# Moving the second chunk's transposes from TensorE to DMA in a fused FFT-mixing and gated-MLP kernel, with two alternating token buffers

## The chip, the cores and the metric

One core of a Trainium2 chip. The metric is the device time of one execution in microseconds (us). An execution that is over 1.5% longer than the fastest of the same kernel in its round is called slow, the others fast: of 15 executions of the kernel before, 12 took 181.61 to 183.95 us and three 184.34 to 186.31 us. Where a profiled execution was itself a slow one, the text says so, and only its local order of events is read from it.

## The reference, cut to what matters

```python
def reference(A_x, A_w_r, A_w_i, B_x, B_w_gate, B_w_up, B_w_down):
    x = A_x                                    # 1 x 2048 x 512, bf16
    xn = _layernorm(x, axis=-1)
    # A: irfft2(rfft2(xn) * (w_r + 1j * w_i));  weights 2048 x 257
    # B: (gelu(xn @ w_gate) * (xn @ w_up)) @ w_down;  512 x 1792 and 1792 x 512
    return x + _A_ref(xn, A_w_r, A_w_i) + _B_ref(xn, B_w_gate, B_w_up, B_w_down)
```

The kernel writes both Fourier transforms as matrix products in stages: a 512-point stage along the features, then 64-point and 32-point stages along the tokens, a product with the filter, and the same backwards. Gate, up and down products of the MLP fill TensorE between these stages.

## The kernel before: the parts that the change and the argument touch

The 2048 tokens are worked on as four chunks of 512. Each chunk is normalised (VectorE, with a power on GpSimd), transposed into `xnT`, combined by four additions and subtractions ("butterflies", VectorE) and multiplied by the 512-point table (`unit_D`, TensorE). The gate and up products need the same `xnT`. Between the 64-point and the 32-point stage each chunk is written to a scratch in DRAM and loaded back (`scr`, `tv`), both by SP's queue.

```python
def trans(m, dcs, jjs, eng="dve"):        # on TensorE: 8 transposes into a PSUM bank, then a copy
    bk = take(1, 0.45, 1.2)
    ...
def trans_dma(m):                         # one DMA transpose of 128 x 2048 fp16 (0.5 MB), SP's queue
    op("sp", lambda e: e.dma_start_transpose(xnT[...], xn...),
       r=[("xn", i) for i in range(4)], w=[("xnT", m, dc, jj) ...], dma=True)
```

Side work hangs on numbered hooks between the gate and up units; a hook is passed after each group of four 128x512 matmuls (0.86 us) and after each product. Loads of constants and weights hang there too, by default on GpSimd's queue:

```python
def load_late(dst, src, keys, also=(), eng="pool"):
    op(eng, lambda e: e.dma_start(dst, src), ..., dma=True, after=[("pe", pr.cnt["pe"])])
...
for i in range(4):                                    # down weights, 1.8 MB
    at(10 + 2 * i, (load_late, wd_sb[...], wdv[...], ...))
at(18, (load_late, be[:], c_be.ap(), ["be"]))         # two small tables
at(19, (load_late, mm[:], c_mm.ap(), ["mm"]))
for s, h0 in enumerate((24, 31, 38, 53, 61, 66, 70, 75)):   # eight sets of filter rows,
    for i, t in enumerate(load_W(s)): at(h0 + i // 2, t)    # half by GpSimd's queue, half by SP's
    at(89 + s // 2 if s > 3 else (47, 48, 51, 58)[s], (keep_256, s))
```

PSUM banks are chosen while the program is built, from an estimate of when each comes free; the choice is fixed in the built kernel:

```python
def take(n, dur, hold=None, ops=1):       # n neighbouring banks
    i = min(range(9 - n), key=lambda i: max(free[i:i + n]))
    ...
```

In the second half, eight groups of 32-point work alternate a unit `unit_B` and `unit_C`.

## Time and profile before

| before | value |
|---|---|
| time, median of 3 | 183.42 us (182.3 to 186.33) |
| span of the profiled execution, granted clock | 181.5 us, full speed in every slice |
| second chunk: transposes | 16 on TensorE, two blocks of 0.46 us, near 25 and 26 us |
| third and fourth chunk: DMA transposes, issue to landing | 7.7 us (issued at 34.74), 6.3 us (46.42) |
| first matmul of the third and fourth chunk's 512-point stage | 44.51 and 54.79 us, late by 1.45 and 0.96 us |
| first 32-point unit; first unit after the eight groups | 74.20; 122.22 us |

How to read it: TensorE sets the end; it is busy for 173.2 of the 181.5 us. A wait of it in the first 55 us is taken to move the end by its own length (my estimate: its row has no gap worth naming behind that), and so the two late stages, with the transposes on TensorE, are what the change goes for.

### The profile page before, as it was taken

The page shows a single profiled execution, that of the slowest core. Times are in us where ns is not written, and L with a number is a line of the kernel's source. Part 1 is how long each engine was busy: PE and PEld are TensorE (multiplying, and loading weights), DVE is VectorE, ACT ScalarE, POOL GpSimd, SP SyncE. Part 2 cuts the span into 40 slices and gives each one's busy share as a digit, 9 for nine tenths or more (in the row PEclk, how much of TensorE's full clock was granted, in tenths as well). Part 3 has the DMA queues.
Part 4 walks back from the last instruction along what each step waited for, and adds up shares of the span by engine and source line. Part 5 has one row for each costly group of instructions (what it writes and reads, how often), then busy time and mean ns, then how long its engine had stood idle before and what let it go on. Part 6 is the DMA issues. An engine that isn't in the chain of part 4 may idle for free.

```text
span 181.5 us, 3815 instructions
## 1 busy us (share of the span) xinstructions
PE 173.2 (95%) x1406; PEld 107.9 (59%) x1406; DVE 132.4 (73%) x331; ACT 93.9 (52%) x158; POOL 54.9 (30%) x107
## 2 busy tenths in 40 slices
PE   7889999997989999999999999999999999999992
PEld 2478654553536556556655656556676767666882
DVE  3496989966649695786876649797877777897552
ACT  3334547763666631475655755336858677632110
POOL 2210171462222426186570000001354625640000
PEclk9999999999999999999999999999999999999999
DMA  3999998698999566469973121394155755552104
GB/s 86 320 270 304 342 280 297 169 234 148 242 167 207 132 158 164 115 166 205 216 188 92 58 61 58 106 249 170 19 99 105 130 115 101 92 86 44 29 5 116
DMA packets 31059, 27.89 MB, mean 154 GB/s; under 512 B 7120, under 2 KB 27984, under 8 KB 30912
## 3 DMA queue, kind: packets, MB, share of 16 engines
q1 hardware_dynamic: 26016, 19.88, 44.6%
q0 software_dynamic: 4272, 7.24, 18.2%
q10 hardware_dynamic: 752, 0.52, 1.1%
q8 instruction: 11, 0.18, 0.4%
q14 instruction: 8, 0.07, 0.1%
HBM read 18.19 MB, written 6.29 MB: 135 GB/s over the span
## 4 chain that ended last, share of the span: by engine, by line
PE 70%; DVE 12%; DMA 11%; SPq 2%; issue 2%; POOL 1%; ACT 0%; DVEq 0%
PE ps L778 23%; PE ps L889 19%; PE ps L874 18%; DMA xnT<-cmx 8%; DMA wu<-in_B_w_up_dram 4%; DVE st L384 3%; SPq L337 2%; PE ps L604 2%; PE ps L632 2%; PE ps L832 2%; DVE hT L895 2%; PE ps L579 2%; DVE cmx L430 1%; DVE arena L740 1%; DVE arena L434 1%
## 5 line engine op out<-in xcount | busy, mean ns | idle before, releaser
L889 PE MATMUL ps<-xnT,wu 128*128 128x512 f16 (+1 forms) x248 | 58.4, 359 | 0.7 <-DMA wu<-in_B_w_up_dram 0.7
L874 PE MATMUL ps<-xnT,wg 128*128 128x512 f16 (+1 forms) x248 | 58.4, 359 | 0.5 <-ACT xnT L1023 0.5
L877 ACT ACTIVATE gl<-ps 128x512 bf16<-128x512 f32 (+1 forms) x62 | 34.4, 556 | 37.5 <-PE ps L874 36.7
L895 DVE TENSOR_TENSOR hT<-ps,gl 128x512 bf16<-128x512 f32 (+1 forms) x62 | 39.2, 635 | 19.9 <-PE ps L889 13.9
L889 PEld LDWEIGHTS ps<-xnT,wu 128*128 128x128 bf16 x248 | 23.1, 98 | 20.4 <-issue 1.2
L874 PEld LDWEIGHTS ps<-xnT,wg 128*128 128x128 bf16 x248 | 23.2, 98 | 15.8 <-issue 1.4
L340 POOL DMA_DIRECT2D wring<-in_A_w_r_dram x32 | 18.4, 609 | 18.1 <-PE ps L874 7.7
L641 POOL COPY tv<-tv 1x128 bf16<-1x128 bf16 x16 | 5.4, 338 | 41.9 <-ACT tv L639 41.8
L778 PE MATMUL ps<-wd,hT 128*128 128x256 bf16 x112 | 14.4, 273 | 0.0
L858 POOL DMA_DIRECT2D x_sb<-tv x16 | 13.2, 865 | 3.4 <-DVE tv L851 2.4
L384 DVE BATCH_NORM_STATS2 st<-x_sb 128x6 f32<-128x512 bf16 x16 | 10.5, 680 | 3.9 <-DMA x_sb<-in_A_x_dram 3.9
L455 ACT ACTIVATE early<-ps 128x512 f16<-128x512 f32 x16 | 9.5, 595 | 7.2 <-PE ps L451 7.2
L590 DVE TENSOR_TENSOR early<-early,wring 128x1024 bf16<-128x1024 f16 x16 | 10.3, 686 | 3.8 <-ACT early L585 3.8
L797 ACT ACTIVATE ps<-ps 128x256 f32<-128x256 f32 x16 | 5.9, 369 | 13.2 <-PE ps L778 13.1
L778 PEld LDWEIGHTS ps<-wd,hT 128*128 128x128 bf16 x112 | 10.7, 98 | 2.5
L392 POOL TENSOR_TENSOR rstd<-vpe,mhalf 128x4 f32<-128x4 f32 (+2 forms) x6 | 5.0, 837 | 21.2 <-DVE vpe L391 21.2
L778 PE MATMUL ps<-arena,xnT 128*128 128x256 f16 x91 | 11.4, 273 | 0.0
L838 ACT ACTIVATE tv<-ps 128x512 bf16<-128x512 f32 x16 | 9.5, 595 | 3.6 <-PE ps L832 3.6
L639 ACT ACTIVATE tv<-ps 128x512 bf16<-128x512 f32 x16 | 9.5, 595 | 3.2 <-PE ps L632 3.2
L585 ACT ACTIVATE early<-ps 128x1024 f16<-128x1024 f32 x8 | 8.2, 1023 | 4.8 <-PE ps L579 4.8
L778 PEld LDWEIGHTS ps<-arena,xnT 128*128 128x128 f16 x91 | 8.6, 98 | 2.3 <-DVE tw L801 0.3
L659 DVE TENSOR_TENSOR x_sb<-ps,tw 128x256 bf16<-128x256 f32 x16 | 6.7, 421 | 2.9 <-PE ps L778 2.6
(118 smaller groups left out, 236.9 us busy)
## 6 DMA issues: line engine op xcount, KB each, us to landing
wring<-in_A_w_r_dram POOLq DMA_DIRECT2D x32, 64.2 KB, 4.0
wring<-in_A_w_i_dram SPq DMA_DIRECT2D x32, 64.2 KB, 3.9
tv<-scr SPq DMA_DIRECT2D x8, 256.0 KB, 5.0
scr<-early SPq DMA_DIRECT2D x8, 256.0 KB, 2.2
wring<-scr SPq DMA_DIRECT2D x4, 512.0 KB, 7.1
x_sb<-tv POOLq DMA_DIRECT2D x16, 128.0 KB, 2.8
scr<-early SPq DMA_DIRECT2D x15, 128.0 KB, 3.5
out_dram<-x_sb SPq DMA_DIRECT2D x28, 64.0 KB, 2.0
```

Source lines behind the costliest of these rows:

```text
L340: op(eng, lambda e: e.dma_start(dst, src), w=list(keys) + list(also), dma=True, after=[("pe", pr.cnt["pe"])])
L384: op("dve", lambda e: e.bn_stats(st[:, j, :], x_sb[:, j, :]), r=[("x", j, 0), ("x", j, 1)], w=[("st", j)])
L455: op("act", lambda e: e.activation(x4.rearrange("p (a c r) -> p a c r", a=2, r=4), bank(bk).rearrange("p (a r c) -> p a c r", a=2, r=4), A ...
L590: op("dve", lambda e, k=k: e.tensor_tensor(pp[i][k], xc[i], W[k][g % 4][:, :, :, 0:256], ALU.mult), r=[("xc", i)] + [key for c in range(2) ...
L639: op("act", lambda e: e.activation(z, bank(bk).rearrange("p (a c) -> p a c", a=4), ACT.Copy, scale=SC_E), r=[("ps", bk)], w=[zk] + (TVK if ...
L778: ins = e.matmul(o, st_(f), mv(f), start=(f == 0 and step in (0, 5)), stop=(f == 6), skip_group_check=True)
L838: op("act", lambda e: e.activation(o2, bank(bk), ACT.Copy), r=[("ps", bk)], w=[ok] + (TVK if j < 2 else []))
L858: op("pool", lambda e: e.dma_start(x_sb[:, j, :], ys, accum_op=ALU.add), r=[yk + (0,), yk + (1,), ("x", j, 0), ("x", j, 1)] + acc(j), w=ac ...
L874: ins = e.matmul(bank(bg)[:, 0:n], wg_sb[:, dc, fc * P:(fc + 1) * P], xnT[:, j0:j0 + len(jjs), dc, :], start=(dc == 0), stop=(dc == 3))
L877: op("act", lambda e: e.activation(gl[k % 3][:, 0:n], bank(bg)[:, 0:n], ACT.Gelu_apprx_tanh), r=[("ps", bg)], w=[("gl", k % 3)])
L889: ins = e.matmul(bank(bu)[:, 0:n], wu_sb[:, dc, fc * P:(fc + 1) * P], xnT[:, j0:j0 + len(jjs), dc, :], start=(dc == 0), stop=(dc == 3))
L895: op("dve", lambda e: e.tensor_tensor(hT[b % 2][:, fc, h0:h0 + n], bank(bu)[:, 0:n], gl[k % 3][:, 0:n], ALU.mult), r=[("ps", bu), ("gl", k ...
```

## The change

The second chunk is transposed by DMA as well. Since the transposes are now closer together, the third chunk is normalised into a second buffer (`twh`, space that is free until later), so that its normalisation needn't wait until the second chunk's transpose has read the first buffer. Each chunk's 512-point stage is moved to the hook where its transpose is expected to have landed: the second chunk's from hook 22 to 27, the third's from 31 to 35, the fourth's from 39 to 40. Two small moves come along: the third filter set from hook 38 to 37, and one 32-point unit (`unit_C` of the fourth group) a hook later.

```diff
+        def xnb(m):
+            return twh.rearrange("p (a d) -> p a d", a=4) if m == 2 else xn
...
         def trans_dma(m):
-            op("sp", lambda e: e.dma_start_transpose(xnT[...], xn.rearrange("p a d -> p (a d)")),
+            op("sp", lambda e: e.dma_start_transpose(xnT[...], xnb(m).rearrange("p a d -> p (a d)")),
...
-        for s, h0 in enumerate((24, 31, 38, 53, 61, 66, 70, 75)):
+        for s, h0 in enumerate((24, 31, 37, 53, 61, 66, 70, 75)):
...
         for m in range(1, 4):
-            a = (5, 15, 23)[m - 1]
-            t = (16, 25, 33)[m - 1]
+            a = (5, 15, 22)[m - 1]
+            n = (10, 20, 27)[m - 1]
+            t = (20, 29, 36)[m - 1]
...
-                at(a + 5 + i // 2, (ln_norm, 4 * m + i))
-            if m < 2:
-                at(t, (trans, m, (0, 1), (0, 1, 2, 3)))
-                at(t + 1, (trans, m, (2, 3), (0, 1, 2, 3), "act"))
-            else:
-                at(a + 6, (trans_dma, m))
+                at(n + i // 2, (ln_norm, 4 * m + i))
+            at(n + 1, (trans_dma, m))
...
-            h = (11, 22, 31, 39)[m]
+            h = (11, 27, 35, 40)[m]
...
-                at(h + (g in (1, 5)), (unit_C, g - 1))
+                at(h + (g in (1, 4, 5)), (unit_C, g - 1))
```

More of the change, by code (lines that the diff above doesn't have):

```diff
@@ L304, in bass_parallel_sum__spectral_gfnet__glu_gated_geglu__prompt_kernel @@
         tw = sb("tw", [P, 2, 512], F32)
+        twh = tw[:].rearrange("p a c -> p (a c)").bitcast(F16)
         dumm = sb("dumm", [P, 512], F16)
@@ L393, in ln_aggr, with xnk @@
                w=[("rstd", j) for j in js])
+        def xnb(m):
+            return twh.rearrange("p (a d) -> p a d", a=4) if m == 2 else xn
+        def xnk(m, a):
+            return ("tw", a // 2, a % 2 == 0) if m == 2 else ("xn", a)
         def ln_norm(j):
-            op("dve", lambda e: e.tensor_scalar(xn[:, j % 4, :], x_sb[:, j, :], ag[:, j, 0:1], rstd[:, j:j + 1], ALU.subtract, ALU.mult),
-               r=[("x", j, 0), ("x", j, 1), ("ag", j), ("rstd", j)], w=[("xn", j % 4)])
+            op("dve", lambda e: e.tensor_scalar(xnb(j // 4)[:, j % 4, :], x_sb[:, j, :], ag[:, j, 0:1], rstd[:, j:j + 1], ALU.subtract, ALU.mult),
+               r=[("x", j, 0), ("x", j, 1), ("ag", j), ("rstd", j)], w=[xnk(j // 4, j % 4)])
         def trans(m, dcs, jjs, eng="dve"):
@@ L419, in trans_dma @@
         def trans_dma(m):
-            op("sp", lambda e: e.dma_start_transpose(xnT[:, 4 * m:4 * m + 4].rearrange("p j d c -> p (j d) c"), xn.rearrange("p a d -> p (a d)")),
-               r=[("xn", i) for i in range(4)], w=[("xnT", m, dc, jj) for dc in range(4) for jj in range(4)], dma=True)
+            op("sp", lambda e: e.dma_start_transpose(xnT[:, 4 * m:4 * m + 4].rearrange("p j d c -> p (j d) c"), xnb(m).rearrange("p a d -> p (a d)")),
+               r=[xnk(m, i) for i in range(4)], w=[("xnT", m, dc, jj) for dc in range(4) for jj in range(4)], dma=True)
         def butter(m, part):
@@ L712, in sum_01 @@
                    after=readers(home + (SK(3) if k == 1 else [])))
-        twh = tw[:].rearrange("p a c -> p (a c)").bitcast(F16)
         def s01k(b, p, k):
```

## The prediction

> **What bounds the kernel now.** I read the page first (busy shares, then the 40 slices), then the chain of waits, then TensorE's timeline and, beside it, those of VectorE and of the SP queue from 12 to 66 us, then the transfers by window.
>
> ```profile
> PE 173.2 (95%) x1406; PEld 107.9 (59%) x1406; DVE 132.4 (73%) x331; ACT 93.9 (52%) x158; POOL 54.9 (30%) x107
> ...
> PE   7889999997989999999999999999999999999992
> ...
> DMA  3999998698999566469973121394155755552104
> ```
>
> TensorE is busy nearly everywhere. From slice 13 (about 55 us) on it has no gap worth naming, so a microsecond saved before that moves the end by a microsecond. What can be saved lies in slices 3 to 12. The DMA row is full up to slice 6, about 32 us. That matters below.
>
> ```profile
> 25.16 0.62 PE L406 MATMUL ps<-ident,cmx 128*128 128x128 f16 x8 [0.24 <-DVE cmx L396]
> ...
> 26.48 0.61 PE L406 MATMUL ps<-ident,cmx 128*128 128x128 f16 x8
> ...
> 42.20 1.03 PE L889 MATMUL ps<-xnT,wu 128*128 128x512 f16 x4
> 44.51 0.23 PE L447 MATMUL ps<-fd,arena 128*128 128x128 f16 x1 [1.28 <-DVE arena L434]
> ...
> 54.79 0.23 PE L447 MATMUL ps<-fd,arena 128*128 128x128 f16 x1 [0.79 <-DVE arena L434]
> ```
>
> In TensorE's timeline (start, length, instruction, idle before it) L406 are the 16 transposes of the second chunk of tokens, L447 the first matmul of a chunk's 512-point stage. Both stages whose tokens come by DMA make TensorE wait. The listed idle is short of the wait, because the pipelined ends are modelled. I use the distance between starts: four 128x512 matmuls start their successor 0.86 us later (41.34 to 42.20), so the unit of 42.20 is done at 43.06, and 44.51 is 1.45 us late.
>
> ```profile
> 34.74 3.39 SPq L420 DMA_TRANSPOSE xnT<-cmx  x1
> ...
> 46.42 2.27 SPq L420 DMA_TRANSPOSE xnT<-cmx  x1
> ```
> ```profile
> 42.49 0.69 DVE L430 TENSOR_TENSOR cmx<-xnT 128x1024 f16<-128x1024 f16 x1 [2.85 <-DMA xnT<-cmx]
> ...
> 52.77 0.69 DVE L430 TENSOR_TENSOR cmx<-xnT 128x1024 f16<-128x1024 f16 x1 [2.58 <-DMA xnT<-cmx]
> ```
>
> So the cause is plain: a DMA transpose takes 7.7 and 6.3 us from its issue, VectorE idles for it, then needs 2.0 us for four butterflies (42.49 to 44.51), and TensorE arrives before that is done.
>
> [...]
>
> **The change, part by part.** I number the places where the program hangs its side work ("hooks"), one after each gate or up unit (four matmuls, 0.864 us) and after each product, and put each on TensorE's timeline.
>
> Removed from TensorE: the transposes. Two blocks of 8 cost 0.46 us each (25.16 to 25.62), 0.91 in all; the first also waited for the normalised tokens (unit of 23.89 done at 24.75, transposes at 25.16), 0.41. From VectorE go 0.67 us, from ScalarE 1.02 us, both then off the path.
>
> Removed by moving: the two waits, 1.45 us before 44.51, and 0.96 before 54.79 (the unit of 52.97 is done at 53.83). The second chunk's own stage waited 0.22 (32.66 to 32.88). Sum of all that can go: 0.91 + 0.41 + 1.45 + 0.96 + 0.22 = 3.95 us. A further 0.27 us wait at 66.8, for a difference of weights on VectorE, may go too, as its producers come earlier relative to TensorE; at most 4.2 us. VectorE's and GpSimd's work for normalisation is the same; only its destination changes for the third chunk.
>
> Now each stage against its transpose, on a timeline without waits. After 24.75 TensorE reaches hook 20 at 28.5, hook 27 at 35.65, hook 35 at 45.0 and, behind the third chunk's 64-point stage, hook 40 at 51.7.
>
> Third chunk: VectorE has its tokens at about 32.7; SP is free at about 33.1 (its four scratch writes took 2.82 us and come a little over 1 us earlier). Plus 7.7 us gives 40.8. Butterflies hang at hooks 31 and 32 (40.4 and after), done near 44.2; the matmuls at 45.0 find them ready. The wait of 1.45 goes. Its own buffer frees nothing else early: the fourth chunk's normalisation comes at hook 27 anyway.
>
> Fourth chunk: tokens near 41.1, landing near 48 to 49, butterflies at hook 38 (48.6) and 39, done near 51.4, against 51.7. No wait, or a few tenths.
>
> Second chunk: tokens at 25.02, as before. The transpose is issued at 25.1, into this:
>
> ```profile
> 25.00:26.00 1.00, 0.84 (x10) 0.66 (x11) 1.00 (x3) 0.55 (x1) 1.00 (x2) 1.00 1.02 251
> ...
> 30.00:31.00 1.00, 1.00 (x18) 0.72 (x18) 1.00 (x2) 0.95 (x2) 0.00 (x0) 1.00 0.94 315
> 31.00:32.00 1.00, 1.00 (x5) 0.42 (x6) 0.97 (x7) 1.00 (x2) 0.35 (x1) 1.00 0.32 109
> ```
> ```profile
> x_sb<-in_A_x_dram SPq DMA_DIRECT2D x1, 256.0 KB, 15.0
> ```
>
> The last two columns of the windows are the DMA share and GB/s: full until 31. The second fence is the first of the last two input loads of SP, issued at 13.84, landing at 28.8; the two have a median of 13.2, so the other took 11.4 and lands near 29.8. In front of the new transpose SP's queue is full until then, and GpSimd's 1.8 MB of down weights (issued from 23.1, landing 8 to 9 us later) take their share. In the two old cases the transpose landed 4.3 to 4.9 us after the scratch writes ahead of it (last issues near 34 and 44.3, 3.6 us each). From 29.8 that gives an estimate of 34.1 to 34.7; with the plain 7.7 it would be 32.8. I take 34.0. After it VectorE runs, by program order, two butterflies (1.28), a statistic (0.60), a product for the up unit (0.60) and the last two butterflies (0.75): 3.2 us, so 37.2, against TensorE's arrival at 35.65. **New wait: about 1.5 us**, in a range of 0.3 to 2.2.
>
> The later stages then slide by the same time on both engines, so it is counted once. Sum: 4.1 - 1.5 = 2.6 us, and a few tenths of noise. 183.42 - 2.7 = **180.7 us**, a ratio of 0.985.
>
> **Rivals.** (a) The third transpose is hidden: it lands by 32.5 and VectorE, busy until 32.7, never waits. For it: the author put 17 hooks between normalisation and matmuls here against 13 and 15 elsewhere, as if measured. Against: the full DMA row. It would give 179.3 to 179.5, just beyond 2%. (b) The queue behind the loads is worse, landing at 36 or later: the gate units of the second chunk, which need the same tokens at hook 27, wait as well, and since VectorE is in order, up products pile up behind the butterflies (it lags TensorE by 3 to 4.4 us already between 17 and 26 us), PSUM banks stay taken, and the gain falls to 1 us or less: 182.5 or more. For it: the input loads took 15 us in this queue. Against: most of their bytes are gone by 25. (c) The gain moves to a later wait: the second half needs the scratch reload of the fourth chunk by hook 59. Before, it was issued at 67.5, landed near 71.4, used at 74.2, 2.8 us to spare. After, the stage is one hook later in the program but SP carries fewer loads ahead of it; I estimate 1 to 2 us to spare. If not, 1 us is lost.
>
> **Range and chances.** The ceiling of 4.2 us is 2.3%, so faster by over 2% needs a new wait under 0.5 us: (a), 0.2. Slower by over 2% would need a loss of over 7 us, for which no part is big enough, or a disturbed run: 0.03. The rest is within 2%. The range is 179.2 (all gone, a lucky run) to 182.3 (b, or a and c together with the spread of 182.3 to 186.3 of the kernel before).
>
> **What would show it.** In the changed kernel: no L406 after 14 us; three DMA transposes on SP, the first at 25.1 landing after 8 to 9.5 us, the others after 6 to 8; VectorE idle 1 to 2 us before the second chunk's first butterfly; TensorE's only wait of over 0.5 us between 20 and 60 us before the second chunk's first 512-point matmul, near 36 to 37; the third and fourth stages without one. Wrong if the first landing is at 32.7 or before (then a), if TensorE's units slow down with no tokens awaited (b), or if a wait appears at the 32-point stage near 70 us (c).

## The result, and the profile after

The changed kernel took 191.76 us (median of 4, 190.42 to 196.62) against 183.31 us for the kernel before on the same chip: a ratio of 1.0465 (95% interval 1.0357 to 1.0574). It is slower by over 2%, outside the predicted range. All ratios here are worked out from the fast runs of both kernels in the same rounds, so they are not quite the ratio of the medians quoted.

The first profiled execution was a slow one (span 194.7 us), so the changed kernel was run again unchanged, as the run r1_again below, whose profiled execution was fast (span 187.9 us). Everything said of the kernel after is read from that one. Its page, 40 slices of 4.7 us:

```profile
PE   7799999509999999999999999999999999999991
...
PEclk9999999965999999999999999999999999999998
DMA  4999999995668856739774212186064665651104
```

There is one hole in TensorE's row, at slices 7 and 8 (counted from 0), where there was none before; in its second half and right behind it, in slices 8 and 9, the granted clock is lowered. The trace's record of the clock has half speed from 39.44 to 46.27 us. The end of TensorE's timeline around it (start, length, instruction, idle before it and what ended it; L455 is the first matmul of a chunk's 512-point stage):

```profile
34.60 1.03 PE L895 MATMUL ps<-xnT,wu 128*128 128x512 f16 x4
41.99 0.29 PE L455 MATMUL ps<-fd,arena 128*128 128x128 f16 x1 [6.36 <-DVE arena L442]
...
42.60 1.91 PE L880 MATMUL ps<-xnT,wg 128*128 128x512 f16 x4
44.31 0.31 PE L455 MATMUL ps<-fd,arena 128*128 128x128 f16 x1
...
46.47 0.22 PE L455 MATMUL ps<-fd,arena 128*128 128x128 f16 x1
```

By the prediction's own measure, the unit of 34.60 is done at 35.46, so the second chunk's stage is 6.53 us late. And the four matmuls at 42.60 take 1.71 us until their successor starts, instead of 0.86. From 41.99 to 46.47 there are two pairs of a 512-point unit and a gate or up unit, 1.19 us each at full clock (before: 45.72 to 46.91); 4.48 - 2.38 = 2.10 us are lost to the lowered clock. The table by windows has the clock itself (third column from the end):

```profile
42.00:44.00 2.00, 2.00 (x8) 1.05 (x9) 2.00 (x4) 0.60 (x1) 0.00 (x0) 0.50 0.95 252
```

What TensorE waits for is VectorE's last butterfly (L442), and VectorE waits for the transpose. First VectorE's timeline, then the SP queue's:

```profile
38.77 0.69 DVE L438 TENSOR_TENSOR cmx<-xnT 128x1024 f16<-128x1024 f16 x1 [6.08 <-DMA xnT<-cmx]
...
41.51 0.42 DVE L442 TENSOR_TENSOR arena<-cmx 128x512 f16<-128x512 f16 x1
```
```profile
24.93 6.61 SPq L428 DMA_TRANSPOSE xnT<-cmx  x1
...
35.33 4.95 SPq L428 DMA_TRANSPOSE xnT<-tw  x1
...
47.36 1.62 SPq L428 DMA_TRANSPOSE xnT<-cmx  x1
```

The transpose of 24.93 landed 13.8 us after its issue, the other two after 6.9 and 4.4 us. From its landing on, all runs as predicted: 3.2 us of VectorE, and the stage begins. The third chunk's stage waits for nothing. The fourth's is about 0.3 us late (its first matmul is at 60.40, with 0.23 us of listed idle); in return a wait of 0.27 us that the kernel before had near 66.5 us is gone, and the two cancel in the sum below.

The whole difference, by the times of the same events in both traces:

| from before to after | us |
|---|---|
| transposes off TensorE (0.91) and old waits gone (0.41 + 1.45 + 0.96 + 0.22) | -3.95 |
| first 512-point gate unit begins earlier in this execution (19.78 to 19.57) | -0.21 |
| new wait before the second chunk's stage | +6.53 |
| lowered clock after it | +2.10 |
| sum: first 32-point unit at 74.20 before, 78.67 after | +4.47 |
| eight 32-point groups: 48.02 before (74.20 to 122.22), 49.12 after (78.67 to 127.79) | +1.10 |
| from there to the last product group: 54.44 in both | 0 |
| after VectorE's last instruction (3.1 before, 3.9 after), not followed up | +0.8 |
| sum: span 181.5 to 187.9 | +6.4 |

The gain came as computed, but for the 0.3 us at the fourth stage. Three things ate it: a landing 4.8 us later than the 34.0 predicted, the clock, and 1.1 us in a place that the change seemed hardly to touch.

### The profile page after: what moved, and what is told of

Read it like the earlier page. It is cut to its first block, busy times and chain, and to the rows that moved or that the text cites. A ratio compares the mean times of both kernels' runs of the same rounds, so it can differ in the third digit from the quotient of the medians.

```text
span 194.7 us, 3785 instructions
## 1 busy us (share of the span) xinstructions
PE 175.4 (90%) x1390; PEld 108.3 (56%) x1390; DVE 132.3 (68%) x330; ACT 93.1 (48%) x157; POOL 53.8 (28%) x107
## 4 chain that ended last, share of the span: by engine, by line
PE 75%; DMA 14%; DVE 4%; SPq 2%; issue 2%; ACT 2%; DVEq 0%
PE ps L784 22%; PE ps L895 21%; PE ps L880 21%; DMA xnT<-cmx 9%; DMA wu<-in_B_w_up_dram 5%; SPq L338 2%; PE ps L612 2%; PE ps L640 2%; PE ps L838 2%; PE ps L587 1%; ACT early L593 1%; DVE hT L901 1%; PE ps L458 1%; PE ps L459 1%; PE ps L455 1%
## 5 line engine op out<-in xcount | busy, mean ns | idle before, releaser
L895 PE MATMUL ps<-xnT,wu 128*128 128x512 f16 (+1 forms) x248 | 59.3, 363 | 1.8 <-DMA wu<-in_B_w_up_dram 1.8
L880 PE MATMUL ps<-xnT,wg 128*128 128x512 f16 (+1 forms) x248 | 59.4, 363 | 1.3 <-DMA wg<-in_B_w_gate_dram 0.7
L784 PE MATMUL ps<-wd,hT 128*128 128x256 bf16 x112 | 14.4, 273 | 0.0
L455 PE MATMUL ps<-fd,arena 128*128 128x128 f16 x16 | 3.8, 236 | 10.1 <-DVE arena L442 10.1
L593 ACT ACTIVATE early<-ps 128x1024 f16<-128x1024 f32 x8 | 8.2, 1022 | 4.8 <-PE ps L587 4.8
```

Source lines behind the costliest of these rows:

```text
L593: op("act", lambda e: e.activation(xc[i].rearrange("p r hh c -> p (r hh c)"), pair(bk), ACT.Copy, scale=SC_B), r=[("ps", bk), ("ps", bk + ...
L784: ins = e.matmul(o, st_(f), mv(f), start=(f == 0 and step in (0, 5)), stop=(f == 6), skip_group_check=True)
L880: ins = e.matmul(bank(bg)[:, 0:n], wg_sb[:, dc, fc * P:(fc + 1) * P], xnT[:, j0:j0 + len(jjs), dc, :], start=(dc == 0), stop=(dc == 3))
L895: ins = e.matmul(bank(bu)[:, 0:n], wu_sb[:, dc, fc * P:(fc + 1) * P], xnT[:, j0:j0 + len(jjs), dc, :], start=(dc == 0), stop=(dc == 3))
```

## The experiments

The question for the first five runs: why did a transpose that takes 4 to 8 us elsewhere take 13.8 us here? The main theory: while a transpose's packets and those of another queue's loads are in flight together, the transpose hardly moves; here GpSimd's down weights (issued from 22.86 on) and the loads behind them are the others. The rivals: the transpose only waits its turn behind SP's own input loads, or one particular load does it, or the moved stages themselves are badly placed.

**r1_again: the change unchanged**, for a fast profile and as the base of the others.

> The change once more, unaltered, for a second trace beside the runs that follow. If its slowness is steady: 190 to 192 us, the first DMA transpose landing 13 us or more after its issue while GpSimd's queue carries the down weights and small loads, TensorE waiting 6 us or more and its granted clock then at 0.5 for some microseconds. If the first trace was an odd one: a landing within 9 us in this trace.

Measured: 190.81 us, ratio 1.0349 (1.0272 to 1.0426); two of the four runs were fast. Its profile is the one above. (r2 to r5 were run before it; their expectations quote the slow first execution, in which TensorE waited 9.9 us.) The record of DMA transfers by window gives the first piece of evidence. From 27 to 29 us (queue, kind: packets, MB, share of the 16 engines' time; then the transpose with its time to landing):

```profile
q0 software_dynamic: 178, 0.66, 98.6%
q1 hardware_dynamic: 7, 0.02, 4.0%
...
xnT<-cmx SPq DMA_TRANSPOSE x1, 13.8
```

q0 is GpSimd's queue, q1 SP's. For two microseconds, 2 us after the transpose was issued, GpSimd's queue has the engines nearly for itself. The seven packets of q1 are not yet the transpose's: five have 4096 bytes and two have 4, the rest of SP's input loads, which landed at 28.34 and 29.31 us. The transpose's own packets, 2048 of 256 bytes, start between 29.65 and 35.81 us (in r11, below, between 27.09 and 30.09). From 29.6 to 32 us, beside the down weights, three packets in five are the transpose's, but they are so small that they carry 0.08 of 0.75 MB:

```profile
q0 software_dynamic: 202, 0.67, 92.7%
q1 hardware_dynamic: 314, 0.08, 18.9%
```

From 33.0 to 34.2 us hardly anything moves in either queue (161 packets of q1, 12 of q0), and why is open. From 34.2 to 35.2 us the transpose has the engines to itself, and half of it passes in this one microsecond:

```profile
q1 hardware_dynamic: 1035, 0.26, 125.4%
```

**r2_second_on_pe: the second chunk back on TensorE**, all the rest of the change kept.

```diff
-            t = (20, 29, 36)[m - 1]
+            t = (16, 29, 36)[m - 1]
-            at(n + 1, (trans_dma, m))
+            if m < 2: (the two blocks of transposes of the kernel before)
+            else:     at(n + 1, (trans_dma, m))
-            h = (11, 27, 35, 40)[m]
+            h = (11, 22, 35, 40)[m]
```

> The second chunk goes back to TensorE transposes at its old places; the third and fourth keep the change's buffer and later stages. If the whole loss comes from the second chunk's DMA transpose, the old waits of 1.45 and 0.96 us before the third and fourth chunk's stages are gone and no new one appears: 181.0 us (ratio 0.987). If moving the stages or the second buffer costs something by itself: 184 or more.

Measured: 185.2 us, ratio 1.0039 (0.9987 to 1.0092). So the loss belongs to the second chunk's transpose by DMA, not to the moved stages. But these alone gain nothing either. In the profiled execution (a slow one) the fourth chunk's transpose was issued only at 46.10, though its tokens were ready at 42.8: SP was busy issuing filter loads and scratch writes. It took 7.3 us, and TensorE's timeline has a new wait:

```profile
56.62 0.23 PE L455 MATMUL ps<-fd,arena 128*128 128x128 f16 x1 [1.82 <-DVE arena L442]
```

**r3_down_late: the down weights later**, from hooks 10 to 16 to hooks 22 to 25.

```diff
-            at(10 + 2 * i, (load_late, wd_sb[...], ...))
+            at(22 + i, (load_late, wd_sb[...], ...))
```

> The change, with the four loads of the down weights (GpSimd's queue, 1.8 MB) moved from hooks 10 to 16 to hooks 22 to 25, behind the issue of the second chunk's transpose. Theory A (the transpose is held up by GpSimd's down weights on the shared DMA engines): it lands within 8 us of its issue and TensorE's wait of 9.9 us before the second chunk's stage falls under 1.5 us, 180 to 182.5 us, unless the later weights now hold up the next transpose. Theory B (it is held up by the input loads ahead of it in SP's own queue): it still lands 12 us or more after its issue, 187 us or more. Theory C (by the small loads of GpSimd that share the engines from 33 to 41 us): little better than the change, 187 or more.

Measured: 191.93 us, ratio 1.0403 (1.0295 to 1.0511). The second chunk's transpose landed after 6.0 us: without the down weights beside it, it is fast. But now they were in flight beside the third chunk's transpose, issued at 34.16, and that one took 21.4 us. TensorE's timeline (a slow execution):

```profile
57.65 0.29 PE L455 MATMUL ps<-fd,arena 128*128 128x128 f16 x1 [11.80 <-DVE arena L442]
```

The wait has moved with the load. A transpose that only stands in line behind SP's input loads wouldn't do that.

**r4_small_late: the small tables and the first two filter sets later**, down weights as in the change.

```diff
-        at(18, (load_late, be[:], ...)); at(19, (load_late, mm[:], ...))
-        for s, h0 in enumerate((24, 31, 37, 53, 61, 66, 70, 75)):
+        at(33, (load_late, be[:], ...)); at(34, (load_late, mm[:], ...))
+        for s, h0 in enumerate((29, 33, 37, 53, 61, 66, 70, 75)):
```

> The change, with the small loads (two constant tables and the first two sets of filter weights) moved from hooks 18, 19, 24 and 31 to hooks 33, 34, 29 and 33; the down weights stay. Theory A (down weights): the transpose still lands 14 us or more after its issue, 189 to 191 us. Theory C (the small loads in GpSimd's queue keep the transpose slow after 33 us): first packets near 32 us as before but all landed by 36 to 37 us, so 183 to 185 us. Theory B (SP's own queue): no change, 190 us.

Measured: 195.43 us, ratio 1.0657 (1.0573 to 1.0741). With the down weights still beside it, the second chunk's transpose took 14.8 us as before, the others 6.7 and 5.1. The small loads are not the ones that hurt the second chunk. That this kernel is slower than the change itself (1.0657 against 1.0349) was not followed up; its profiled execution, a slow one, has a further wait of 2.54 us for the reload from the scratch, at 86.50.

**r5_both_late: r3 and r4 together.**

> Both of the two foregoing moves together, so that GpSimd's queue is empty while the second chunk's transpose is in flight. Theory A or C: it lands 5 to 7 us after its issue, TensorE's wait there is under 0.5 us, 179.5 to 181.5 us unless the later transposes are held up in turn. Theory B: it lands 9 us or more after its issue, 183 us or more.

Measured: 191.43 us, ratio 1.0367 (1.0267 to 1.0467). The transposes took 4.6, 11.8 and 10.5 us: the first is as fast as any, the next two are beside the delayed loads and make TensorE wait 2.69 and 1.95 us (a slow execution). So it is no one load, but whichever loads of the other queue are in flight at that time; and moving them later in the same queue only chooses the victim.

**r6_one_queue: the same bytes, on SP's own queue.** Down weights and tables are issued by SP at the same hooks, and the first three filter sets, of which half goes by GpSimd, move behind the transposes.

```diff
-            at(10 + 2 * i, (load_late, wd_sb[...], wdv[...], [...]))
-        at(18, (load_late, be[:], c_be.ap(), ["be"])); at(19, (load_late, mm[:], c_mm.ap(), ["mm"]))
-        for s, h0 in enumerate((24, 31, 37, 53, ...)):    # keep_256 at 47, 48, 51, 58
+            at(10 + 2 * i, (load_late, wd_sb[...], wdv[...], [...], (), "sp"))
+        at(18, (load_late, be[:], c_be.ap(), ["be"], (), "sp")); at(19, (load_late, mm[:], ..., (), "sp"))
+        for s, h0 in enumerate((39, 43, 46, 53, ...)):    # keep_256 at 52, 53, 54, 58
```

> The change, with the down weights and the two constant tables issued by SP at their old hooks, in the transposes' own queue (same bytes, same places in the program), and the first three sets of filter weights moved behind the last transpose, so that GpSimd's queue is empty while any transpose is in flight. Theory A (packets of another queue, interleaved with those of the transpose, hold it up): all three land within 9 us of their issue, no wait of TensorE over 1 us from 20 to 60 us, 179 to 181.5 us. Theory D (the bytes in flight matter, whichever queue carries them): the first transpose still needs 12 us or more, 186 us or more. Theory B (SP's own backlog holds it up): worse than the change, 191 us or more.

Measured: 186.45 us, ratio 1.018 (1.01 to 1.026), so half of the loss of r1_again is gone. The first transpose landed after 9.6 us. SP was busy with the transpose's issue from 25.16 to 31.23 us, so only the first of the four weight loads was ahead of it; the other three and the tables went out at 31.28 and later, behind it. The other two transposes, with no other queue's load beside them, landed after 4.5 and 4.3 us. Two waits are left in TensorE's timeline:

```profile
37.98 0.23 PE L455 MATMUL ps<-fd,arena 128*128 128x128 f16 x1 [1.87 <-DVE arena L442]
...
74.70 0.47 PE L587 MATMUL ps<-tv,be 64*64 64x256 f16 x8 [2.06 <-DMA tv<-scr]
```

The second is the prediction's rival (c): the reload of the fourth chunk from the scratch is late for the first 32-point unit. From 76 to 78 us the granted clock was 0.50.

**r7_fill: the change, with 36 needless matmuls where TensorE waits**, to tell the wait from the clock.

```diff
+        at(27, (warm, 36))
```

> The change, with 36 dummy matmuls of 128x512 (0.216 us each, 7.8 us) ahead of the second chunk's first 512-point matmul, where TensorE waits anyway. If the lowered clock after the long wait (0.5 from 43 to 53 us in the first trace) is a cost of its own: no lowered clock, about 2.5 us saved, 188 us. If the wait alone is the loss and the clock costs nothing: 190 to 192 us as the change.

Measured: 189.51 us, ratio 1.0354 (1.0292 to 1.0416), as r1_again. In TensorE's timeline:

```profile
36.47 7.93 PE L380 MATMUL ps<-dumm 128*128 128x512 f16 x36
44.31 0.23 PE L455 MATMUL ps<-fd,arena 128*128 128x128 f16 x1
...
45.51 0.22 PE L455 MATMUL ps<-fd,arena 128*128 128x128 f16 x1
```

The stage begins 2.32 us later than in r1_again (44.31 against 41.99), because in this execution the transpose was issued 1.0 us later and took 15.1 us; the clock stays at full speed in every slice, the units come every 1.19 us again, and the span is 188.1 against 187.9 us. So the lowered clock after the wait costs about 2.1 us, as the sum above has it. From the stage to the first 32-point unit it is 34.60 us here and 36.68 us there. In this execution the later landing hides the gain; that the median, too, stayed above the 188 us expected was not followed up.

**r10_act_queue: r6, but by ScalarE's queue.** The same loads at the same hooks as in r6, with "act" for "sp".

> As r6_one_queue, but the down weights and the two tables are issued by ScalarE's queue instead of SP's; GpSimd's queue is empty while the transposes are in flight. Theory A1 (packets of any second queue hold a transpose up): the first transpose needs 12 us or more, as the 14.8 us with the down weights alone on GpSimd's queue, 188 us or more. Theory A2 (it is GpSimd's queue that does it): it lands within 10 us, as the 9.6 us with the same loads in SP's queue, 184 to 187 us (the wait for the reload near 75 us stays).

Measured: 192.27 us, ratio 1.0508 (1.0449 to 1.0567). The first transpose took 14.4 us, and TensorE waited 6.68 us for it. So it is not something special to GpSimd's queue: both second queues that were tried do it. The comparison with r6 (9.6 us) is less clean than it looks. The bytes and the hooks are the same, but ScalarE issued all six loads by 29.0 us, while in r6 five of the six went out behind the transpose. It shows that these loads cost the transpose when a second queue sends them at that time; whether the same bytes ahead of it in SP's own queue would cost as much was not tested.

**r8_before_filters_late: the kernel before, with the first three filter sets behind the transposes.** If loads beside a transpose slow it, the two waits of the kernel before have the same cause.

```diff
-        for s, h0 in enumerate((24, 31, 38, 53, ...)):    # keep_256 at 47, 48, 51, 58
+        for s, h0 in enumerate((38, 42, 46, 53, ...)):    # keep_256 at 52, 53, 54, 58
```

> The kernel before, with only the first three sets of filter weights moved from hooks 24, 31 and 38 to 38, 42 and 46, behind its second DMA transpose, and their last columns kept later. Theory A: its two transposes, which took 7.7 and 6.3 us, land in about 5 us, the waits of 1.45 and 0.96 us shrink below 0.3 us each, and the time falls by about 2 us to 181.3 us. If those loads don't matter for a transpose: 183.4 us.

Measured: 185.45 us instead of the 181.3 expected, ratio 1.0108 (1.0021 to 1.0195). The transposes landed after 4.2 and 3.7 us instead of 7.7 and 6.3, and both old waits are gone. But the delayed sets now stand before a later table (a slow execution):

```profile
80.78 0.63 PE L604 MATMUL ps<-early,cmx 64*64 64x256 bf16 x16 [2.21 <-DMA cmx<-c_cm]
```

**r9_before_loads_between: the kernel before, with its loads in the gaps between the transposes.**

```diff
-        at(18, (load_late, be[:], ...)); at(19, (load_late, mm[:], ...))
-        for s, h0 in enumerate((24, 31, 38, 53, ...)):    # keep_256 at 47, 48, 51, 58
+        at(38, (load_late, be[:], ...)); at(37, (load_late, mm[:], ...))
+        for s, h0 in enumerate((28, 36, 40, 53, ...)):    # keep_256 at 47, 50, 53, 58
```

> The kernel before, with GpSimd's loads placed between its two DMA transposes instead of on them: filter sets 0 to 2 at hooks 28, 36 and 40 (from 24, 31, 38), the two constant tables at 37 and 38 (from 18, 19), the kept columns of sets 1 and 2 at hooks 50 and 53. If transposes with no traffic of GpSimd's queue land in 4 to 4.5 us (4.2 and 3.7 in the run with the filters moved behind them), both old waits of TensorE (1.45 and 0.96 us) go and, as nothing is pushed into the 64-point stages later, 181 us or a ratio of 0.985 to 0.99. If a new wait for a later load or a reload takes their place: 183 us or more, with that wait in the trace.

Measured: 181.61 us over 22 runs, ratio 0.9921 (0.9894 to 0.9948): faster than the kernel before, with the old waits gone (transposes of 3.8 and 6.1 us). Not all of the 2.41 us arrive: this execution's first gate unit began 1.34 us later than that of the kernel before (21.12 against 19.78), and the first 32-point unit has a wait of its own:

```profile
73.92 0.41 PE L579 MATMUL ps<-tv,be 64*64 64x256 f16 x8 [0.71 <-DVE x_sb L659]
```

**r11_alone_in_flight: the change with its loads out of the transposes' way.** Down weights by SP at hooks 12 to 15, behind the transpose in the same queue; tables and filter sets between or behind the transposes.

```diff
-            at(10 + 2 * i, (load_late, wd_sb[...], wdv[...], [...]))
-        at(18, (load_late, be[:], ...)); at(19, (load_late, mm[:], ...))
-        for s, h0 in enumerate((24, 31, 37, 53, ...)):    # keep_256 at 47, 48, 51, 58
+            at(12 + i, (load_late, wd_sb[...], wdv[...], [...], (), "sp"))
+        at(39, (load_late, be[:], ...)); at(38, (load_late, mm[:], ...))
+        for s, h0 in enumerate((36, 40, 44, 53, ...)):    # keep_256 at 52, 55, 58, 59
```

> The change as it was meant: each transpose alone on the DMA engines or behind loads of its own queue. Down weights issued by SP at hooks 12 to 15, right behind the second chunk's transpose; the two tables on GpSimd's queue at hooks 38 and 39; filter sets 0 to 2 at 36, 40 and 44; kept columns at 52, 55 and 58. If other queues' packets are the whole cause: the first transpose lands within 7 us of its issue at 25 us, the others within 9 and 6, no wait of TensorE over 0.5 us from 20 to 60 us, and the ceiling worked out before (3.9 us) is reached if the reload near 70 us is not late: 179.5 to 181 us, a ratio of 0.98 to 0.99. If a new wait appears there (as the 2.06 us with the one-queue run): 182 to 184 us. If the first transpose still takes over 9 us: 184 us or more, and something else holds it.

Measured: 183.67 us over 22 runs, ratio 1.0023 (0.9994 to 1.0051). The transposes took 4.8, 7.5 and 5.2 us, and no wait over 0.23 us is left between 20 and 60 us. With no other queue's load beside it and SP's input loads out of the way, the first transpose moved like this, from 28.7 to 29.7 us:

```profile
DMA packets 1133, 0.29 MB, mean 290 GB/s; under 512 B 1133, under 2 KB 1133, under 8 KB 1133
...
q1 hardware_dynamic: 1133, 0.29, 127.7%
```

That is close to the 1035 packets that r1_again moved from 34.2 to 35.2 us. So once nothing is beside it, the transpose keeps about the same pace in both; what differs is the time before. Not every standstill comes from the mixing, though: from 27.6 to 28.6 us this transpose, too, moved little (152 packets in all, with no other queue at work). Nearly all of the change's loss is undone. But there is no gain, since rival (c) is back:

```profile
73.12 0.41 PE L587 MATMUL ps<-tv,be 64*64 64x256 f16 x8 [1.80 <-DMA tv<-scr]
```

**r12_third_set_behind_reload: r11 with the third filter set behind that reload.**

```diff
-        for s, h0 in enumerate((36, 40, 44, 53, ...)):    # keep_256 at 52, 55, 58, 59
+        for s, h0 in enumerate((36, 40, 50, 54, ...)):    # keep_256 at 52, 55, 62, 64
```

> As r11_alone_in_flight, with the third set of filter weights moved from hook 44 to 50 (the fourth from 53 to 54, their kept columns to 62 and 64), so that SP issues the last scratch reload, which TensorE waited 1.80 us for at 73 us, without four filter loads ahead of it. If those loads delayed the reload: it is issued near 63.5 us instead of 66.4, the wait is gone, and the time is 1.5 to 2 us less, 181 to 182 us or a ratio of 0.985 to 0.993. If the reload is held by its own chain (the scratch writes it waits for): the wait stays over 1 us and the time is that of r11, ratio 1.00.

Measured: 181.93 us over 22 runs, ratio 0.994 (0.9914 to 0.9967). The wait for the reload shrank to 1.06 us, at 71.01. The first 32-point unit begins 3.19 us earlier than before (0.46 us of it because this execution's first gate unit began earlier), but the stretch of the eight groups takes 49.12 us, the same 1.1 us more as in r1_again and r11. In r9, which is the kernel before in this part, it takes 48.02.

**r13_fourth_unit_back: r12 with the moved 32-point unit put back.** The theory: the later hook of the change costs the 1.1 us.

```diff
-                at(h + (g in (1, 4, 5)), (unit_C, g - 1))
+                at(h + (g in (1, 5)), (unit_C, g - 1))
```

> As r12_third_set_behind_reload, with the fourth product of the 32-point stage (unit C of index 3) back at its old hook; the only other difference from r12 is none. In every traced kernel with the change's later hook, TensorE needs 1.1 us more between its first 64-point units of the second kind and the first inverse unit (49.12 us against 48.02 in the kernel before and in the run built on it). If that later hook is the cause: those 48.02 us again, ratio 0.988, about 180.7 us. If it comes from elsewhere in the change: 49.1 us still, ratio 0.994.

Measured: 183.06 us, ratio 1.0053 (1.0024 to 1.0082). The theory falls: the stretch became longer, 49.88 us. (The ratio rose by 0.011, about 2 us; the 0.76 us of this stretch and 0.48 us more of waiting for the reload don't make up all of that, and the rest was not followed up.) TensorE's timeline has the wait that the later hook had partly hidden, and it is for ScalarE:

```profile
93.34 0.63 PE L612 MATMUL ps<-early,cmx 64*64 64x256 bf16 x16 [1.22 <-ACT early L593]
```

**r14_fourth_chunk_earlier: r13 with the fourth chunk's stage one hook earlier**, against the wait for the reload.

```diff
-            t = (20, 29, 36)[m - 1]
+            t = (20, 29, 35)[m - 1]
-            h = (11, 27, 35, 40)[m]
+            h = (11, 27, 35, 39)[m]
```

> As r13_fourth_unit_back, with the fourth chunk's butterflies and 512-point matmuls one hook earlier (35 and 39 instead of 36 and 40), as its transpose now lands early. In r12 TensorE waited 1.06 us at 71 us for the last scratch reload, which hangs behind that chunk's stage. If the reload is held by its own chain, that wait shrinks by the length of a hook, about 0.9 us: ratio 0.983 to 0.986, 180 us. If the new place makes TensorE wait for the fourth chunk's butterflies instead: no gain on r13.

Measured: 182.63 us, ratio 1.0028 (0.9997 to 1.0058), 0.0025 below r13 and inside its interval. The wait for the reload is gone, but the stage now comes before its butterflies are done (0.87 us, at 50.95), and the eight groups take 49.43 us. So the change's later hook for this stage was right by its own measure: what is taken off one wait returns in the other.

**r15_banks_apart: r12 with two units in other PSUM banks.** Why does ScalarE hold up `unit_C`? L593 is ScalarE's emptying of the banks of `unit_B`, just before. I repeated the program's own choice of banks: before, the pairs of the fifth `unit_B` and the `unit_C` that follows it are 4-5 and 2-3, and of the next two 1-2 and 4-5, all apart; in the changed kernel they are 3-4 and 2-3, then 1-2 and 0-1, so that each time the two share a bank. The stages in new places and the transposes that no longer take banks have shifted the rotation. The edit keeps r12 and forbids these two units the pair of the last `unit_B`:

```diff
         def unit_C(g):
+            b0 = lastB[0]                     # set in unit_B
+            kept = free[b0:b0 + 2]
+            if g in (3, 4):
+                free[b0:b0 + 2] = [1e12, 1e12]
             bk = take(2, 0.46)
+            if g in (3, 4):
+                free[b0:b0 + 2] = kept
```

> This is the kernel of r12, with one thing changed: the 32-point product unit of the third and the fourth group takes a pair of PSUM banks that does not overlap the pair that ScalarE is then emptying. Theory (bank collision): in every kernel derived from the change, these two units take a bank of the pair just filled by the previous unit and wait for its eviction, about 1.0 us each, of which the change's later hook hides part; so the time from the first 32-point unit to the first unit that follows the eight groups falls from 49.12 us to 48.0 us, as in the kernel before, and the ratio from 0.994 to about 0.988 (about 180.8 us). Rival (the later hook or the order of work on VectorE costs it): the stretch stays at 49.1 us and the ratio at 0.994.

Measured: 181.36 us over 24 runs, ratio 0.9915 (0.9884 to 0.9946). The profiled execution was a slow one: a wait of 4.37 us for the reload, and a lowered clock after it, fall on the first two groups and spoil the whole stretch (49.93 us). From the third `unit_C` on its clock is at full speed, and there it can be compared: until the first unit after the groups it is 34.46 us before (from 87.76), 35.56 in r1_again (from 92.23) and in r12 (from 84.57), and 34.69 here (from 90.15). So 0.87 of the 1.10 us are gone. The chain of waits, first of r1_again, then of r15, at the fifth and sixth group (start, length, what the end waited for; L612 and L622 are the same line, `unit_C`):

```profile
97.55 1.03 ACT early L593
98.72 0.63 PE ps L612 x16
...
103.34 1.03 ACT early L593
104.50 0.63 PE ps L612 x16
```
```profile
95.08 0.34 PE ps L590 x8
96.29 0.56 PE ps L622 x16
100.31 0.34 PE ps L590 x8
101.62 0.56 PE ps L622 x16
```

ScalarE has left the chain. That the shared bank was the cause is shown, then, by the trace; in the times the step from 0.994 to 0.9915 is of the right sign, less than half of the expected size and within the intervals. The remaining 0.23 us go with the later hook: r2, too, has that hook and, by the same repetition, these two units in banks apart (2-3 and 6-7, then 6-7 and 2-3), and the same stretch takes it 34.69 us (from 89.56 to 124.25), with ScalarE out of the chain. No run takes that hook away with the banks apart.

## Why the prediction was wrong, point by point

**What bounds the kernel, and what goes.** Right. The two waits, the transposes and the small waits went, 3.95 us by the same events in r1_again; the third stage waited for nothing and the fourth for about 0.3 us.

**The second chunk's landing: the step that failed.** The text takes the old cases' 4.3 to 4.9 us after the work ahead of it, from the end of SP's backlog at 29.8, and comes to 34.0. Measured: 38.77. The backlog itself was right: SP's last input load landed at 29.31 in r1_again. What failed is the time after it, 9.4 us instead of 4.3 to 4.9; in r11, with no other queue's loads beside it, it was 1.8 us (28.80 to 30.63). The text treated GpSimd's 1.8 MB as traffic that takes "their share". What the runs showed in its place: beside a second queue's loads the transpose moves little (0.08 of 0.75 MB from 29.6 to 32 us), and r3, r5, r6 and r10 turn the length of a transpose between 4.6 and 21.4 us by nothing but when, and by which queue, the loads are issued. I even had the hint: in the kernel before, the transposes took 7.7 and 6.3 us, and I took that for their nature. In r8, with the filter loads behind them, they took 4.2 and 3.7 us. The 3.2 us of VectorE after the landing were right: 38.77 + 3.2 = 41.97, and the stage began at 41.99. Of the signs that the text named, the one wait over 0.5 us came at its place but 5 us late, and the other two transposes took 6.9 and 4.4 us where 6 to 8 were expected.

**A term that was missing: the clock.** The longer wait was followed by about 4 us of work at half clock (41.99 to 46.27 us in r1_again), 2.1 us lost, by the sum and by r7. When the clock falls is not settled by these traces: it fell to 0.50 after listed idle of 1.95 us (r5), 2.06 us (r6) and 2.21 us (r8), and not after 1.80 us (r11), 1.87 us (r6) or 2.69 us (r5), so the idle time alone doesn't decide it. The range's argument that no part is big enough to lose 7 us counted only waits that the profile before could show.

**A second missing term: the PSUM banks.** "Later stages slide by the same time" left out that moving work changes which banks the later units get; 1.1 us, of which r15 takes back 0.87.

**The rivals.** (a), the hidden transpose, is what r11 and r12 make of the change, but only with the loads moved. (b), landing at 36 or later, is what happened, with the wrong loss: I wrote 182.5 or more and put the end of the range below that, while my own 3.2 us and TensorE's arrival at 35.65 give 3.6 us of wait for a landing at 36 and 6.3 us for one at 38.77. The products did stand behind the butterflies: in r1_again VectorE ran none between 32.04 and 40.59 us, though the up units of 32.87 and 34.60 were done by 35.46. (c), the late reload, did not show in r1_again, whose long wait hid it, but in r6, r11 and r12, among others, with 2.06, 1.80 and 1.06 us.

**Where the gain is.** The best versions are r9, 0.9921, the old kernel with its loads between the transposes, and r15, 0.9915, the change with loads and banks put right. Their intervals overlap. So the saving that the change sought lies mostly in where the loads are, and the transposes taken off TensorE add nothing that could be measured. What stays open is why the transpose moves so little beside a second queue's loads (0.08 of 0.75 MB from 29.6 to 32 us of r1_again): SP's own issue of the first transpose took 6.61 us in r1_again and 2.83 us in r11 (and 6.07 us in r6, where no other queue was at work), so part of the starved time may be packets not yet issued rather than packets kept waiting. The records don't tell the two apart. A further part of the 13.8 us was overlooked: the semaphore of a transpose rises in 16 steps, and in r1_again 15 of them had come by 37.05 and the last at 38.75. In the six profiled executions in which the last step of the second chunk's transpose lagged by 0.9 to 1.9 us (the first of the change, r1_again, r4, r6, r7, r10), a packet of 16 KB of the queue that the record calls "instruction" had started 0.4 to 0.9 us before the first step; in the others (r3, r5, r11 to r15) there was no such packet, and the lag was 0.01 us. No run tests this.

## What to carry to other kernels

Before moving a transpose to DMA, list what every other queue has in flight from its issue to its need (here the second chunk's took 13.8 us beside GpSimd's loads, 14.4 us beside ScalarE's and 4.8 us with neither), and take the duration of a transpose only from a place where nothing runs beside it (with the filter loads behind them, 4.2 and 3.7 us in r8; with the loads beside them, 7.7 and 6.3 us before); put bulk loads behind it in the same queue (r11), or between the transposes (r9). Work out the loss of the bad rival as carefully as the gain of the good one, and add the clock to it when TensorE would stand for some microseconds (here 2.1 us after a wait of 6.53 us). After any move of units, compare stretches that the change did not mean to touch: a fixed rotation of PSUM banks can put a new wait far behind it (here two waits for an eviction of 1.03 us, 0.87 of the 1.10 us lost there).
